# A hand-ordered attention and MLP kernel: GpSimd operations made to wait for VectorE's two-operand sums, one batch's q load issued by ScalarE, and a new written order

## The chip, the cores and the metric

The kernel runs on one core of a Trainium2 chip. The metric is the device time of one execution in microseconds (us), taken as the median of several runs. A core has five instruction queues that run side by side and meet at semaphores: TensorE (PE; its weight loads are listed as PEld), VectorE (DVE), ScalarE (ACT), GpSimd (POOL) and SyncE (SP). SP only issues transfers here; POOL and ACT can issue them too. Each queue works strictly in its own order.

## The reference, cut to what matters

```python
# q, k, v: (8 batches, 8 heads, 576 positions, 64)
kv  = einsum('bhsd,bhse->bhde', k, v)            # no softmax
o   = einsum('bhsd,bhde->bhse', q, kv)
x   = o / sqrt(mean(o*o, -1) + 1e-6) * g_norm    # then heads side by side: (8, 576, 512)

a1  = alpha1 * x + beta1
u   = x + lam * einsum('ts,bsd->btd', w_tok, a1) # mixes positions
a2  = alpha2 * u + beta2
out = u + lam * (maximum(a2 @ w_ch1, 0) @ w_ch2) # 512 -> 2048 -> 512
```

## The kernel before, in words

**Stages of one batch.** A batch b (0 to 7) is cut into four tiles of 128 positions, c = 0 to 3, and a tail of 64 positions; the tails of two batches share a tile, c = 4. The stages, by function:

- `load_kv` (L1393) and `load_q` (L1383): k and v by POOL's queue (L1395, L1399), q in four pieces by SP's queue (L1387) into the buffer `qs`, each after the landing that `landing` holds for the batch before.
- `kv` (L628): the k-v products on PE (L634, L640), gathered by ACT (L651) and DVE (L653).
- `qt_steady` (L1403): four pieces of q are transposed by DVE (L1405) and copied by ACT (L1408) to `qt`.
- `norm` (L717): PE multiplies `qt` by the k-v product (L725); ACT squares (L692), DVE sums (L695), ACT takes the root (L698), DVE inverts (L701), multiplies (L703) and writes x to `xm` (L710, or `xt` for a tail). POOL writes the bf16 tile `rm` (L713); for a tail DVE writes `rtl` (L708).
- `tok` (L805) and `tok_tail`: PE mixes positions (L808, L853) and needs all five tiles of `rm` and `rtl`; DVE adds the result to x (L818).
- `a2_dma` (L887): POOL rounds the tile to bf16 (`a2b`, L896; for batch 1 L905), and SP turns it by a transposing DMA (L909) into `a2m` (tail: `a2l`).
- `ch1` (L1018) and `ch1_tail`: the first product of the MLP on PE (L1020, L1034), with the rectifier on ACT (L913, L1042, L1051).
- The second product: `ch2` (L1075, PE L1081, DVE L1263 or L1257, POOL L1266) for batches 0 and 1; `strassen` (L1149) for the others. There DVE makes sums of two bf16 operands that both lie in SBUF (`sums`, `sums_late`, all through L1104), PE multiplies (L1142), ACT copies a partial result (`keep`, L1172), POOL adds it to x (L1175), DVE adds the last part (`last_add`, L1180), and the tile is stored (L1193, L1188). Batches 6 and 7 have such sums in their first product too (`pair`, L961, L983, L987).
- Once: `fold_w2` multiplies w_ch2 by lam (L1071), four slices by DVE and four by POOL; `fold_w1` (L1062) and `weight_sums` (L1104) follow on DVE.

**Order and waits.** Every operation gets a number as it is made. `ORDER` lists these numbers in the order in which they are put out, `a:3` naming the PSUM bank and `a+b` weaving two PE operations; so it sets the order of each of the five queues. `GATES` holds extra waits: `{774: 872}` makes operation 774 wait until 872 has ended. All other waits follow from what is read and written.

**Numbers that the text uses.** 237 to 240: the q load of batch 2. 390, 392, 394, 396 and 391, 393, 395, 397: its four transposes on DVE (L1405) and copies on ACT (L1408). 475, 479, 481, 483: rectifiers of batch 1 on ACT. 491: the first rectifier of batch 1 after the position mixing. 465, 467, 469: DVE's slices of `fold_w2`; 468: POOL's last; 379: POOL's last L1266. 1224: the first `keep` sum of batch 5 on POOL. 1227 to 1230: the four `sums_late` of batch 5 on DVE. 1285, 1301: `rm` tiles of batch 7 on POOL. 1231, 1242: `last_add` of batch 5. 1235, 1239: its other `keep` sums. 1309 and 1308: x and `rtl` of batch 7's tail. 1310: its first `tok`. 1085, 1087: the last two transposes of q of batch 6. 530 to 533: `fold_w1`. 563: the last L1257 of batch 1. 1577, 1590, 1594: the three `keep` sums of the tails, the last work of POOL; 1583: the last sum of L1104; 1567: the last `last_add` of batch 7 but the tails; 1597: the tails' L1180 that waits for 1594; 1575: a product of the tails.

Of the kernel before, what the change touches and what calls it, by code (L numbers as in the profile page):

```python
# [10 lines left out]
ACT = mybir.ActivationFunctionType  # L11
# [343 lines left out]
def bass_transnormer_attn__then__resmlp_affine_kernel(  # L355
# [15 lines left out]
    with ExitStack() as stack:  # L371
        P = Prog(nc, stack)
# [36 lines left out]
        a2b = sb("a2b", [128, 5, DM], BF16)  # L409
# [45 lines left out]
        def dcost(n, ns):  # L455
            return n * ns / 16000.0, float(ns)
# [13 lines left out]
             w=["idb"])  # L470
# [1080 lines left out]
```

## Time and profile before

| | before |
|---|---|
| median of 3 runs | 331.49 us (331.32 to 331.92) |
| the profiled execution | 332.1 us |
| its span, first to last instruction | 330.3 us |
| PE busy | 320.9 us (97%) |
| DVE busy | 252.1 us (76%) |
| ACT busy | 175.5 us (53%) |
| POOL busy | 146.4 us (44%) |
| granted TensorE clock | 1.0 throughout |

Durations in the text are of the profiled execution; what it says of runs is said of the median. Matmuls are pipelined, so the busy time of PE counts the drain of each; how far apart their starts lie is the better measure of whether it is held up. In a timeline the columns are start, time taken, queue, line, operation, tiles out<-in and shape, how many neighbours are merged in the row, and in brackets the idle time of the queue before it and what ended it. In the list of waits the three numbers are total us, times, and the longest.

### The profile page before, as it was taken

The numbers are of one execution on the slowest core, as the hardware profiler recorded it, in microseconds if no ns is written. First come the engines' busy times: TensorE is split into PE (matmuls) and PEld (weight loads), VectorE is DVE, ScalarE is ACT, GpSimd is POOL, SyncE is SP. The second block draws the span as 40 slices with busy tenths as digits, with TensorE's granted clock in tenths as the row PEclk, the third lists the DMA queues.
The fourth block names the chain that finished last, engine by engine and source line by source line (L and its number), as shares of the span: only waits on it lengthen the run. The fifth ranks groups of instructions, "written<-read, shape, count | busy, mean of one in ns | idle before, by whom it ended". The sixth has DMA issues, their size and how long they took to land.

```text
span 330.3 us, 6148 instructions
## 1 busy us (share of the span) xinstructions
PE 320.9 (97%) x2427; PEld 219.3 (66%) x2457; DVE 252.1 (76%) x443; ACT 175.5 (53%) x363; POOL 146.4 (44%) x147
## 2 busy tenths in 40 slices
PE   7999999998999999999999999999999899999996
PEld 7777664453766546786579874787658484557884
DVE  3596078775999998978985499789999677978534
ACT  5584672237734453619842585832784068873011
POOL 3599127899163473443258043564243600003232
PEclk9999999999999999999999999999999999999999
DMA  7999997999932896599059952596500250000314
GB/s 247 333 242 259 215 241 189 190 158 218 237 144 74 168 276 120 98 306 189 31 66 240 257 93 43 85 310 138 130 0 3 47 161 1 2 0 2 127 43 150
DMA packets 108532, 48.15 MB, mean 146 GB/s; under 512 B 82061, under 2 KB 101717, under 8 KB 108504
## 3 DMA queue, kind: packets, MB, share of 16 engines
q1 hardware_dynamic: 81520, 26.24, 33.8%
q0 software_dynamic: 26800, 21.38, 32.7%
q8 instruction: 19, 0.31, 0.4%
q10 hardware_dynamic: 184, 0.14, 0.2%
q14 instruction: 9, 0.07, 0.1%
HBM read 38.82 MB, written 9.44 MB: 146 GB/s over the span
## 4 chain that ended last, share of the span: by engine, by line
PE 71%; DVE 14%; ACT 5%; DMA 4%; issue 2%; SPq 2%; POOL 2%; DVEq 0%
PE ps L1142 21%; PE ps L1020 17%; PE ps L808 7%; PE ps L961 7%; PE ps L1081 6%; PE ps L1034 4%; PE ps L725 3%; DMA qs<-in_q_dram 2%; DVE ps L703 2%; POOL a2b L905 2%; DMA w<-in_k_dram 2%; PE ps L634 2%; ACT hh L913 1%; DVE small L695 1%; DVE qp L1405 1%
## 5 line engine op out<-in xcount | busy, mean ns | idle before, releaser
L1020 PE MATMUL ps<-a2m,w 128*128 128x512 bf16 x372 | 96.6, 385 | 0.6 <-DVE xm L1257 0.2
L713 POOL TENSOR_TENSOR rm<-xm,la_bc 128x512 bf16<-128x512 f32 x28 | 36.7, 1314 | 64.0 <-DVE xm L710 63.9
L1020 PEld LDWEIGHTS ps<-a2m,w 128*128 128x128 bf16 x384 | 35.9, 97 | 38.3 <-DVE xm L1257 0.6
L913 ACT ACTIVATE hh<-ps,b 128x512 bf16<-128x512 f32 x72 | 47.7, 685 | 13.1 <-PE ps L1020 9.4
L1175 POOL TENSOR_TENSOR xm<-xm,tmp 128x512 f32<-128x512 f32 x18 | 23.9, 1342 | 54.1 <-ACT tmp L1172 54.1
L725 PE MATMUL ps<-kvc,qt 128*128 128x128 f32 (+1 forms) x140 | 42.1, 404 | 1.4 <-ACT qt L1408 1.4
L1142 PE MATMUL ps<-w,hh 128*128 128x256 bf16 x344 | 40.2, 273 | 0.0
L1142 PEld LDWEIGHTS ps<-w,hh 128*128 128x128 bf16 x344 | 33.5, 98 | 5.4 <-issue 0.4
L1081 PE MATMUL ps<-w,hh 128*128 128x512 bf16 x138 | 36.5, 385 | 0.1
L634 PE MATMUL ps<-vr,kr 128*128 128x128 f32 x112 | 34.6, 410 | 0.0
L1172 ACT ACTIVATE tmp<-ps 128x512 f32<-128x512 f32 (+1 forms) x21 | 11.9, 566 | 38.4 <-PE ps L1142 38.4
L695 DVE TENSOR_REDUCE small<-sq 128x8 f32<-128x512 f32 (+1 forms) x35 | 23.5, 675 | 10.7 <-ACT sq L692 10.5
L808 PE MATMUL ps<-rm,wt 128*128 128x512 bf16 x106 | 29.1, 382 | 1.2 <-DVE rtl L708 1.1
L725 PEld LDWEIGHTS ps<-kvc,qt 128*128 128x128 f32 (+1 forms) x140 | 27.3, 196 | 4.1 <-ACT qt L1408 2.4
L896 POOL CAST a2b<-xm 128x512 bf16<-128x512 f32 x24 | 16.3, 678 | 30.8 <-DVE xm L818 30.8
L692 ACT ACTIVATE sq<-ps 128x512 f32<-128x512 f32 (+1 forms) x35 | 20.6, 596 | 16.1 <-PE ps L725 15.9
L1180 DVE TENSOR_TENSOR xm<-ps,xm 128x512 f32<-128x512 f32 x24 | 16.4, 686 | 15.7 <-PE ps L1142 8.2
L703 DVE TENSOR_TENSOR ps<-ps,small 128x512 f32<-128x512 f32 (+1 forms) x35 | 24.0, 692 | 0.5
L634 PEld LDWEIGHTS ps<-vr,kr 128*128 128x128 f32 x112 | 22.4, 200 | 1.5
L913 ACT ACTIVATE hh<-ps 128x512 bf16<-128x512 f32 x32 | 17.4, 601 | 10.6 <-PE ps L1020 10.4
L1408 ACT ACTIVATE qt<-qp 128x576 fp32r<-128x576 f32 x24 | 16.1, 683 | 13.0 <-DVE qp L1405 13.0
L1081 PEld LDWEIGHTS ps<-w,hh 128*128 128x128 bf16 x144 | 13.4, 97 | 13.8 <-issue 0.4
(199 smaller groups left out, 616.8 us busy)
## 6 DMA issues: line engine op xcount, KB each, us to landing
out_dram<-xm SPq DMA_DIRECT2D x32, 256.0 KB, 2.8
kr<-in_k_dram POOLq DMA_DIRECT2D x7, 1024.0 KB, 6.4
vr<-in_v_dram POOLq DMA_DIRECT2D x7, 1024.0 KB, 7.9
qs<-in_q_dram SPq DMA_DIRECT2D x24, 288.0 KB, 4.8
w<-in_moe_w_ch_dram POOLq DMA_DIRECT2D x8, 512.0 KB, 11.0
xm<-in_q_dram SPq DMA_DIRECT2D x8, 288.0 KB, 5.4
qs<-in_v_dram SPq DMA_DIRECT2D x4, 288.0 KB, 6.2
w<-in_k_dram SPq DMA_DIRECT2D x4, 288.0 KB, 6.2
```

The source lines that it names most:

```text
L634: P.mm("fill", 128, [lambda e, t=t, c=c, h=h, o=128 * (h % 4): e.matmul(t.ap()[:, o:o + 128], kr4[:, h, c:c + 2, :].rearrange("p c d -> p ...
L695: P.op("DVE", dve(n), lambda e: e.tensor_reduce(out=st, in_=sq[rs, s3, 0:nst, :], axis=AX.X, op=ALU.add), r=[("sq", s3)], w=[("sm", s4)])
L703: P.op("DVE", dve(n), lambda e: e.tensor_tensor(out=grp(ps()), in0=grp(ps()), in1=st[..., None].to_broadcast([rs.stop - rs.start, nst, DH] ...
L713: P.op("POOL", pool(n), lambda e: e.tensor_tensor(out=r, in0=x.rearrange("p h e -> p (h e)"), in1=la, op=ALU.mult), r=xks + ["la"], w=rks)
L725: P.mm("fill", 128, [lambda e, p=p: e.matmul(dst(p), qt[:, p, cs], kvc[:, i, p, :], start=(p == 0), stop=(p == 3)) for p in range(4)], r=[ ...
L808: P.mm("fill", 512, [lambda e, sc=sc: e.matmul(t.ap(), wt[:, sc if sc < 4 else tw(b), 128 * c:128 * c + 128], rsrc(b, sc, al), start=(sc = ...
L913: P.op("ACT", act(512, 0 if f is None else 1), lambda e: e.activation(dst, t.ap(), ACT.Relu, bias=0.0 if f is None else b1[:, f:f + 1]), r ...
L961: P.mm("main", 512, [lambda e, i=i: e.matmul(t.ap(), lhs[:, i, 128 * x + o:128 * x + o + 128], rhs[:, i, :], start=(first and i == 0), sto ...
L1020: P.mm("main", 512, [lambda e, dj=dj: e.matmul(t.ap(), w1[:, dj, 128 * fj:128 * fj + 128], a2m[:, b % 2, dj, :], start=(dj == 0), stop=(dj ...
L1081: P.mm("main", 512, [lambda e, fj=fj, t=t, c=c: e.matmul(t.ap(), (ht[:, fj, 128 * c:128 * c + 128] if c < 4 else hl[:, fj, :]), w2[:, fj, ...
L1142: P.mm("main", 256, [lambda e, c=c, fj=fj: e.matmul(t.ap()[:, 256 * c:256 * c + 256], at[:, fj, 128 * c:128 * c + 128], rhs(fj), start=(fi ...
L1175: P.op("POOL", pool(256 * n), lambda e, cs=cs, f=f: e.tensor_tensor(out=X[:, cs, f], in0=X[:, cs, f], in1=two(tmp[:, s]), op=ALU.add), r=x ...
```

## The change

Three things. `GATES` gets 40 entries: 39 operations of POOL (`keep` sums, `rm` tiles, `a2b` tiles, a slice of `fold_w2`, three L1266) each wait for the end of a DVE operation with two operands in SBUF that stands near them in the order (in one case an L987 with one operand), and the q load of batch 2 (237) waits for the landing of batch 1's third transposed tile (298). That q load is issued by ACT's queue instead of SP's. `landing` no longer keeps the landing of tile c = 3 or of a tail: later loads of k, v and q wait for tile c = 2. And `ORDER` is new from 238 on. POOL's DMA issues and DVE's other operations get no new wait.

```diff
@@ ORDER (from here to the end; only the first and a later stretch are shown)
-297 292 353:7 302 307 303 369 308 298 357 309 304 383:1+373 310 381:2+361 374 370 238 384+365 237
-239 382+490:3+496:0 366 240 462 464 491 470:4 367 385+486:5 463 476:7 388 399 378 471 389 488:3
...
+297 292 353:7 302 307 238 303 369 308 298 357 309 304 383:1+373 310 381:2+361 374 237 370 239
+384+365 240 382+490:3+496:0 366 462 464 491 470:4 367 385+486:5 463 476:7 388 399 378 471 389
...
@@ GATES
-    260, 399: 275, 586: 585, 587: 585, 588: 585, 589: 585, 747: 746, 748: 746, 749: 746, 750:
-    746, 940: 939, 941: 939, 942: 939, 943: 939, 1093: 1092, 1094: 1092, 1095: 1092, 1096:
-    1092}
+    260, 237: 298, 371: 465, 375: 465, 379: 467, 399: 275, 456: 654, 460: 654, 468: 467, 586:
+    585, 587: 585, 588: 585, 589: 585, 597: 656, 605: 651, 613: 651, 621: 656, 632: 657, 636:
+    652, 640: 652, 644: 652, 697: 703, 708: 703, 747: 746, 748: 746, 749: 746, 750: 746, 774:
+    872, 801: 873, 878: 884, 940: 939, 941: 939, 942: 939, 943: 939, 959: 911, 986: 1036, 990:
+    1037, 994: 1037, 1043: 1048, 1093: 1092, 1094: 1092, 1095: 1092, 1096: 1092, 1104: 1047,
+    1112: 1047, 1151: 1334, 1224: 1230, 1277: 1218, 1301: 1230, 1328: 1332, 1505: 1451, 1516:
+    1511, 1520: 1511, 1541: 1537, 1556: 1571, 1577: 1583, 1590: 1583, 1594: 1583}
@@ a2_dma
-            landing[b] = [P.dma(
+            o = P.dma(
                 "SP", "t%d" % c, 0.7, lambda e: e.dma_start_transpose(dst, a2b[:, c]),
-                r=[("a2b", c)], w=dk, issue=0.6)]
+                r=[("a2b", c)], w=dk, issue=0.6)
+            if c < 3:
+                landing[b] = [o]
@@ load_q
-                P.dma("SP", "q%d" % g, dcost(2304, 13.5), lambda e, hp=hp, j=j, g=g: e.dma_start(
+                P.dma("ACT" if b == 2 else "SP", "q%d" % g, dcost(2304, 13.5), lambda e, hp=hp, j=j, g=g: e.dma_start(
```

In the new order, on each queue: on ACT the four q issues stand behind the last L823 of batch 1 and ahead of 491, and rectifiers 481 and 483 go behind 395 and 397. On DVE 1308 goes ahead of 1309; the reciprocals L701 of batch 7's last two tiles stand just ahead of 1230, on which 1224 waits; 1242 goes ahead of batch 7's five L818; 1085 and 1087 go ahead of an L818 each; 530, 531, 533 and 563 go earlier among batch 3's `norm`; 1580 goes ahead of 1567. On SP three stores of batch 0 and 1 go in between and behind the q load of batch 3 instead of all behind it; some stores elsewhere change places with q loads. On POOL 1239 goes ahead of 1235, the keep of batch 4 ahead of batch 6's `rm`, one k load of batch 6 behind two `keep` sums, and loads change places among themselves. On PE some twenty products change places with a neighbour, the tails' 1575 going ahead of two products of batch 7.

123 rows, old and new, of the table ORDER are left out of this document.

## The prediction

> **What bounds the kernel now.** I read the page first (busy shares), then the list of waits for PE, then the timeline around each gap of PE, then what led to it in the chain of waits and the other queues' timelines.
>
> ```profile
> span 330.3 us, 6148 instructions
> PE 320.9 (97%) x2427; PEld 219.3 (66%) x2457; DVE 252.1 (76%) x443; ACT 175.5 (53%) x363; POOL 146.4 (44%) x147
> ```
>
> TensorE is the bound: 97% busy. The change takes no work from it. So only its gaps can be won, and the few per cent that are idle cap the gain. From the list of waits, those of PE that lie in the reordered part:
>
> ```profile
> PE ps L725 <- ACT qt L1408: 1.4, 2, 1.2
> PE ps L808 <- DVE rtl L708: 1.1, 1, 1.1
> PEld ps L1034 <- DMA a2l<-a2b: 0.3, 1, 0.3
> ```
>
> The timeline of PE at its four gaps, each with the row before it:
>
> ```profile
> 80.69 0.81 PE L1020 MATMUL ps<-a2m,w 128*128 128x512 bf16 x3
> 82.74 0.33 PE L725 MATMUL ps<-kvc,qt 128*128 128x128 f32 x1 [1.25 <-ACT qt L1408]
> ```
> ```profile
> 113.85 1.04 PE L1020 MATMUL ps<-a2m,w 128*128 128x512 bf16 x4
> 115.04 0.61 PE L1020 MATMUL ps<-a2m,w 128*128 128x512 bf16 x2 [0.15 <-DVE xm L1257]
> ```
> ```profile
> 205.17 1.03 PE L1020 MATMUL ps<-a2m,w 128*128 128x512 bf16 x4
> 206.37 0.33 PE L725 MATMUL ps<-kvc,qt 128*128 128x128 f32 x1 [0.17 <-ACT qt L1408]
> ```
> ```profile
> 255.10 1.04 PE L1142 MATMUL ps<-w,hh 128*128 128x256 bf16 x8
> 257.27 0.60 PE L808 MATMUL ps<-rm,wt 128*128 128x512 bf16 x2 [1.13 <-DVE rtl L708]
> ```
>
> The bracketed idle time is short of the loss, since each row ends with a drain. An L1020 starts every 0.216 us (three in 0.81 us, of which one lasts 0.38), an L1142 every 0.11 (eight in 1.04, one lasting 0.27). So PE could have gone on at 81.34, 114.72, 206.04 and 255.97. It went on at 82.74, 115.04, 206.37 and 257.27: **holes of 1.40, 0.32, 0.33 and 1.30 us**, 3.35 in all. That is the ceiling that I can name.
>
> **Part 1: GpSimd's 39 waits.** No engine gets more work. What they can win is DVE time: L1104 beside POOL's sums. First one group of L1104 (ns: shortest, median, longest), then PE's busy time in the stretch with its longest (span, sum of PE), then the timelines of DVE and POOL around the hole at 257.
>
> ```profile
> L1104 DVE TENSOR_TENSOR hh<-hh,hs x12: 412/683/4128, 138.7 to 323.5; 128x1024 bf16<-128x1024 bf16 x10, 128x512 bf16<-128x512 bf16 x2
> ```
> ```profile
> 118.00:150.00 32.00, 32.00 (x227) 21.84 (x226) 26.97 (x38) 15.47 (x27) 14.24 (x15) 1.00 0.91 193
> ```
> ```profile
> 249.67 0.69 DVE L1104 TENSOR_TENSOR hh<-hs,hh 128x1024 bf16<-128x1024 bf16 x1
> 250.28 2.36 DVE L1104 TENSOR_TENSOR hh<-hh,hs 128x1024 bf16<-128x1024 bf16 x2
> ```
> ```profile
> 250.00 1.49 POOL L1175 TENSOR_TENSOR xm<-xm,tmp 128x512 f32<-128x512 f32 x1 [2.22 <-ACT tmp L1172]
> 254.28 1.27 POOL L713 TENSOR_TENSOR rm<-xm,la_bc 128x512 bf16<-128x512 f32 x1 [2.79 <-DVE xm L710]
> ```
> ```profile
> 254.98 0.69 DVE L1180 TENSOR_TENSOR xm<-ps,xm 128x512 f32<-128x512 f32 x1
> 255.68 0.69 DVE L710 TENSOR_TENSOR xt<-ps,g_bc 64x512 f32<-64x512 f32 x1
> 256.30 0.69 DVE L708 TENSOR_TENSOR rtl<-ps,e_bc 64x512 bf16<-64x512 f32 x1
> ```
>
> A sum of 0.683 us (median) takes up to 4.128 beside POOL. But that one, at 139, lies in a stretch in which PE is busy for 32.00 of 32.00 us, and is worth nothing. Of the collisions only the one at 250 ends in a hole. Two sums starting 0.61 apart (249.67 to 250.28) would take 0.61 + 0.69 = 1.30; the row says 2.36: **1.06 us lost**, with POOL's 1224 running at 250.00 to 251.49. With the wait, 1224 starts behind 1230, which now ends at 252.64 - 1.06 + 0.20 (one reciprocal moved ahead of it) = 251.8. 1224 then ends at 251.8 + 1.27 = 253.1. What stands behind it on POOL is 1301, which was ready at 254.28, and is ready 1.06 earlier, 253.2: POOL is just free. It ends at 254.5. 1231 on DVE reads 1224's result at 254.98 - 1.06 = 253.9: no wait. The tail's `rtl` (1308), the last thing that PE waits for, ended at 256.99; less 1.06, less 0.62 for the place that it changes with 1309, that is 255.3. PE came 0.28 behind it (256.99 to 257.27), so it could go on at 255.6, and reaches the place at 255.97. The hole closes: **-1.30**; without the exchange of 1308 and 1309 it would be -1.06, and nothing if POOL's 1301 were late.
>
> The other waits have one answer each by group. The slice 468 of `fold_w2` waits for 467, and 379 stands behind it; both feed work that DVE reaches later. The `rm` and `a2b` waits before 250 end in tiles for which PE does not wait in the list above (its L808 waits only for DVE's `rtl`). Cost 0, bounded above by one POOL instruction, 1.27 us, where a tile were the last. At the end of the kernel there is no cover:
>
> ```profile
> 321.31 0.69 DVE L1180 TENSOR_TENSOR xm<-ps,xm 128x512 f32<-128x512 f32 x1 [1.06 <-PE ps L1142]
> ...
> 325.58 0.96 DVE L1180 TENSOR_TENSOR xt<-ps,xt 128x256 f32<-128x256 f32 x2 [1.36 <-POOL xt L1175]
> ```
> ```profile
> 323.95 1.59 POOL L1175 TENSOR_TENSOR xt<-xt,tmp 128x256 f32<-128x256 f32 x2 [1.02 <-ACT tmp L1172]
> ```
>
> 1567 (321.31) moves about 0.43 later, because product 1575 goes ahead of it on PE. Behind it are three half-size sums, 0.33 apart, so 1583 ends near 323.4. Now 1577, 1590 and 1594 follow back to back at 0.72 each: the last ends at 325.65 instead of 325.54. 1597 and PE's last product wait for that: **+0.10** (between 0 and 0.4).
>
> **Part 2: the q load of batch 2 by ACT's queue.**
>
> ```profile
> 60.38 5.24 SPq L909 DMA_TRANSPOSE a2m<-a2b  x4
> 65.66 1.27 SPq L909 DMA_TRANSPOSE a2l<-a2b  x1
> 66.97 5.31 SPq L1387 DMA_DIRECT2D qs<-in_q_dram  x4
> ```
> ```profile
> DMA to landing us min/median/max: 2.4/2.5/4.3
> ```
> ```profile
> 68.99 0.60 ACT L913 ACTIVATE hh<-ps 128x512 bf16<-128x512 f32 x1 [6.37 <-PE ps L1020]
> 71.81 0.38 ACT L651 ACTIVATE kvo<-ps 64x256 f32<-64x256 f32 x1 [2.21 <-PE ps L640]
> ```
> ```profile
> 70.65 6.86 DMA qs<-in_q_dram
> ...
> 80.09 1.46 ACT hh L913 x3
> 81.55 1.15 ACT qt L1408 x2
> ```
>
> The four issues stood on SP behind five transposing DMAs of L909 (the line below the SP rows is the issue-to-landing time of L909). The new wait is for the third: issued near 60.38 + 2 x 1.31 = 63.0, landed 2.5 later, 65.5. So they begin 1.45 us sooner than 66.97. The last piece took 6.86 us from 70.65 (chain of waits), as the next k and v loads came in on POOL; begun at 69.2 it lands at 76.1 with the same 6.86, and sooner if it is clear of them, instead of 77.5. On ACT rectifiers 481 and 483 leave the stretch that ends at 81.55 + 1.15 = 82.70 (three take 1.46, so 0.49 each): it ends at 81.7 even if the load lands no sooner, and at 80.3 or before with the earlier landing. PE comes there at 81.34. **-1.40**; -1.0 with the order alone.
>
> Price on ACT: it stands at the issues from 65.5 to 65.5 + 5.31 = 70.8 where it had 6.37 us idle before 68.99. Behind them are 491, ending at 71.4, and L651, not ready before 71.81. PE needs 491's bank again for its sixth `ch1` tile; the fourth ends with the L640 that released 71.81, the fifth takes 4 x 0.216, so near 72.5. Covered by 1.1 us. SP is free of the four; what is next there, q of batch 3, waits for the DVE transposes.
>
> **Part 3: loads wait for tile 2 instead of the last tile.** They begin one or two transposing DMAs (1.31 us each) sooner, and then share the engines with transposes that are still under way, whose landing goes from 2.5 to 4.3 us at worst. A PE wait for a transposed tile appears once in the list above, 0.3 us. Gain 0, cost between 0 and 1.8 us; I take 0, as that one wait is in batch 7, which no load follows.
>
> **Part 4: the order.** 1085 and 1087 each go ahead of an L818 on DVE, 0.6 us, more than the third hole: **-0.33**. 563 goes ahead of two steps of `norm`, 0.7 us, more than the hole at 114.72: **-0.30** (0 if DVE is later by as much for another reason).
>
> Such a reason would be `fold_w1`, just ahead of 563:
>
> ```profile
> 112.85 0.94 DVE L1062 TENSOR_SCALAR w<-w,ab 128x2048 bf16<-128x2048 bf16 x1
> ```
> ```profile
> 112.13 1.17 POOL L1395 DMA_DIRECT2D vr<-in_v_dram  x1
> ```
>
> The two ran side by side, and POOL's DMA issues get no wait. The Trainium skill ("SBUF — State Buffer", "Who interferes with whom") has a rule that speaks against the change here: a VectorE `tensor_scalar` can hold both ports that it shares with GpSimd, and then not only GpSimd's sums but also the descriptors of a DMA issued by GpSimd exclude it. By that rule this collision stays, and the term would be 0 instead of -0.30. The row neither bears it out nor excludes it, as no L1062 ran alone.
>
> The some twenty exchanges on PE have no row; bounds: 0 and another hole such as the largest, 1.4. I take **+0.3**, the size of the small holes, which are the usual ones here.
>
> **Sum:** -1.40 - 1.30 - 0.33 - 0.30 + 0.10 + 0.30 = -2.93 us, against the profiled execution's 332.1, which is 0.6 above the median. From 331.49: **328.6 us**.
>
> **Rivals.**
> - *The first hole stays.* The q pieces land no sooner and DVE or ACT work fills the stretch before `norm`. For it: DVE has `fold_w2` slices there. Against it: the order alone shortens ACT's stretch. 328.6 + 1.4 = 330.0 us.
> - *The waits only move the hole: no change.* POOL goes 1224, 1301, 1239 without a pause from 251.8, to 255.7 at best and 256.4 if 1224 and 1301 take 1.49 and 1.7; DVE's 1242 (there at about 256) now stands ahead of batch 7's five L818 and waits for 1239, and the a2l landing behind them is the one that PE waits for at 269 (0.3). If 1301 comes late on POOL, the hole at 257 opens again (1.30), and if 1239 is a POOL sum later than that allows (1.27), batch 7's L818 come later by it: 328.6 + 1.30 + 1.27 = 331.2 us.
> - *Slower: ACT is held by the issues.* Four q issues took far longer beside k and v loads:
>
> ```profile
> 115.39 9.29 SPq L1387 DMA_DIRECT2D qs<-in_q_dram  x4
> 213.97 11.01 SPq L1387 DMA_DIRECT2D qs<-in_q_dram  x4
> ```
>
>   On ACT every rectifier of batch 1 stands behind them. Up to 6.4 us PE feels nothing (71.9, then 491, against 72.5). Beyond that it loses one for one: at 9.29 us it is 2.9, which eats the whole gain, and that is the point from which it decides; at 11.01 it is 4.6, and 328.6 + 4.6 = 333.2 us. Against it: the next k and v loads stand on POOL behind batch 2's k-v products on PE, and the same four took 5.31 in this place.
>
> **How the numbers follow.** Forecast 0.62, first hole stays 0.12, no change 0.13, slower 0.13. A measurement of this kernel tells about 0.2%, 0.66 us. So faster 0.74, same 0.13, slower 0.13. The forecast's own range is 327.7 (the new order costs nothing and also closes gaps of 0.1 to 0.2 that I did not count) to 329.8 (+1.4 instead of +0.3). The range goes on to 331.3, with the first two rivals in it, and leaves out the third.
>
> **What would show it.** Right: no PE gap over 0.3 us at the first `norm` of batch 2 and at `tok` of batch 7; the two sums at 250 in 1.3 us; no L1104 over 1.1 us; ACT's four issues in 5 to 6 us. Wrong: a new PE wait on ACT's L913 near 72, on L1408 near 81, or on L808 for POOL's `rm`; a DVE wait for POOL's L1175 that feeds batch 7; transposes landing after 4 us with PE behind them.

## The result, and the profile after

The changed kernel takes 328.56 us (median; 328.33 to 329.46) where the kernel before takes 331.40 us (331.02 to 331.92): ratio 0.9919, 95% interval 0.9898 to 0.9941, so 2.8 us less. The head of the page of the changed kernel (span, then busy time by engine):

```profile
span 326.6 us, 6188 instructions
...
PE 321.1 (98%) x2457; PEld 219.4 (67%) x2457; DVE 242.8 (74%) x443; ACT 175.6 (54%) x363; POOL 141.5 (43%) x147
```

PE does the same work in a shorter span. VectorE is busy for 9.3 us less (252.1 before) and GpSimd for 4.9 less (146.4 before) with the same number of instructions each: the groups that shrink are the sums and roundings that no longer run into each other. VectorE's part alone is three times what the kernel gained. From the list of PE's waits:

```profile
PE ps L464 <- DVE fil L463: 1.1, 1, 1.1
PE ps L811 <- DVE rtl L711: 0.4, 1, 0.4
```

The first is the start of the kernel and was there before. The second is what is left of the hole at 257 us; the wait for `qt` is gone. PE's timeline at the four places where the prediction saw holes:

```profile
77.75 3.40 PE L1025 MATMUL ps<-a2m,w 128*128 128x512 bf16 x15
80.80 0.41 PE L728 MATMUL ps<-kvc,qt 128*128 128x128 f32 x1
...
111.64 4.58 PE L1025 MATMUL ps<-a2m,w 128*128 128x512 bf16 x20
...
201.86 1.89 PE L1025 MATMUL ps<-a2m,w 128*128 128x512 bf16 x8
203.52 0.33 PE L728 MATMUL ps<-kvc,qt 128*128 128x128 f32 x1
...
252.24 0.82 PE L1147 MATMUL ps<-w,hh 128*128 128x256 bf16 x6
253.41 1.04 PE L811 MATMUL ps<-rm,wt 128*128 128x512 bf16 x4 [0.36 <-DVE rtl L711]
```

The first three are closed: each row goes on where the one ahead of it ends, without a bracket. The fourth is half closed. Its cause stands in the timelines of DVE, then POOL, then ACT:

```profile
244.66 0.69 DVE L1109 TENSOR_TENSOR hh<-hh 128x1024 bf16<-128x1024 bf16 x1
246.18 0.69 DVE L1109 TENSOR_TENSOR hs<-hh 128x1024 bf16<-128x1024 bf16 x1 [0.83 <-ACT hh L918]
246.91 1.29 DVE L1109 TENSOR_TENSOR hh<-hs,hh 128x1024 bf16<-128x1024 bf16 x2
248.12 0.68 DVE L1109 TENSOR_TENSOR hh<-hh,hs 128x1024 bf16<-128x1024 bf16 x1
...
252.66 0.69 DVE L711 TENSOR_TENSOR rtl<-ps,e_bc 64x512 bf16<-64x512 f32 x1
```
```profile
249.93 1.27 POOL L1180 TENSOR_TENSOR xm<-xm,tmp 128x512 f32<-128x512 f32 x1 [5.24 <-DVE hh L1109]
251.26 1.27 POOL L716 TENSOR_TENSOR rm<-xm,la_bc 128x512 bf16<-128x512 f32 x1
```
```profile
245.46 0.69 ACT L918 ACTIVATE hh<-ps,b 128x512 bf16<-128x512 f32 x1
```

The collision is gone: no sum takes more than 0.69 us, POOL's 1224 (249.93) comes behind 1230 and 1301 right behind 1224. But the new order puts 1220 (246.18) ahead of 1227, and 1220 waits 0.83 us for ACT's rectifier 1184. With `rtl` PE gets its last operand at 253.35.

**How the runs are compared.** The executions differ by up to 2.3 us in the first 20 us, where PE waits for the first loads. All kernels here are the same up to PE's product 369 (a `ch2` product of batch 0; it starts at 62.35 us in the profile of before, at 61.99 in that of the changed kernel, and between 61.58 and 63.86 in the experiments), and behind it two kernels agree within about 0.01 us up to the first place that their edit touches. So each trace is measured from the start of 369 to the end of the span: 330.27 - 62.35 = 267.92 us before, 326.62 - 61.99 = 264.63 after, **-3.29**. The medians say -2.84. By medians every kernel here stands worse against before than by its trace, by 0.4 to 1.8 us, and before has one profiled execution, 0.6 above its median. The zero of this measure is therefore uncertain by a microsecond or so. The single executions of e4 and e5, which keep the old order, do follow that of before within 0.1 us outside the places that the text names for them, so these steps are no drift; but each kernel has one trace, and the reading by tenths is that of one execution each.

| kernel | order | GpSimd's waits | q of batch 2 | from 369 to the end, us | against before | ratio of whole times, 95% |
|---|---|---|---|---|---|---|
| before | old | none | SP | 267.92 | | |
| changed | new | 39 | ACT | 264.63 | -3.29 | 0.9898 to 0.9941 |
| e1 | new | none | ACT | 267.36 | -0.56 | 0.9989 to 1.0024 |
| e2 | new | 39 | SP | 265.12 | -2.80 | 0.9908 to 0.9952 |
| e13 | new | none | SP | 267.66 | -0.26 | 1.0003 to 1.0033 |
| e4 | old | 37 | SP | 266.59 | -1.33 | 0.9934 to 0.9981 |
| e5 | old | none | ACT | 266.94 | -0.98 | 0.9965 to 1.0016 |
| e11 | old | 37 | ACT | 264.97 | -2.95 | 0.9938 to 0.9979 |
| e6 | new | 9 | ACT | 264.85 | -3.07 | 0.9890 to 0.9947 |
| e3 | new, 1227 first | 39 | ACT | 264.07 | -3.85 | 0.9893 to 0.9939 |
| e10 | new, 1227 first | 10 | ACT | 264.25 | -3.67 | 0.9904 to 0.9955 |
| e9 | new, landing as before | 39 | ACT | 264.85 | -3.07 | 0.9915 to 0.9962 |
| e12 | new | 39 | ACT, 238 later | 264.77 | -3.15 | 0.9927 to 0.9971 |
| e8 | new | 39 | ACT, all later | 273.37 | +5.45 | 1.0136 to 1.0219 |

### The profile page after: what moved, and what is told of

Same layout as the page of the kernel before. It is cut to its first block, busy times and chain, and to the rows that moved or that the text cites. A ratio compares the mean times of both kernels' runs of the same rounds, so it can differ in the third digit from the quotient of the medians.

```text
span 326.6 us, 6188 instructions
## 1 busy us (share of the span) xinstructions
PE 321.1 (98%) x2457; PEld 219.4 (67%) x2457; DVE 242.8 (74%) x443; ACT 175.6 (54%) x363; POOL 141.5 (43%) x147
## 4 chain that ended last, share of the span: by engine, by line
PE 87%; DVE 6%; ACT 2%; DMA 2%; SPq 1%; issue 0%; POOL 0%; POOLq 0%
PE ps L1025 26%; PE ps L1147 20%; PE ps L1086 10%; PE ps L811 10%; PE ps L966 7%; PE ps L1039 4%; PE ps L728 3%; PE ps L637 2%; DMA qs<-in_v_dram 2%; PE ps L856 1%; DVE hh L1109 1%; DVE small L779 1%; PE ps L593 1%; SPq L480 1%; PE ps L876 1%; ACT hh L918 1%
## 5 line engine op out<-in xcount | busy, mean ns | idle before, releaser
L1025 PE MATMUL ps<-a2m,w 128*128 128x512 bf16 x384 | 98.5, 384 | 0.0
L716 POOL TENSOR_TENSOR rm<-xm,la_bc 128x512 bf16<-128x512 f32 x28 | 35.5, 1274 | 59.4 <-DVE xm L713 52.5
L1180 POOL TENSOR_TENSOR xm<-xm,tmp 128x512 f32<-128x512 f32 x18 | 23.1, 1293 | 62.2 <-DVE xm L992 33.3
L1147 PE MATMUL ps<-w,hh 128*128 128x256 bf16 x344 | 41.0, 273 | 0.0
L1086 PE MATMUL ps<-w,hh 128*128 128x512 bf16 x144 | 37.7, 385 | 0.0
L811 PE MATMUL ps<-rm,wt 128*128 128x512 bf16 x112 | 30.2, 382 | 0.4 <-DVE rtl L711 0.4
L899 POOL CAST a2b<-xm 128x512 bf16<-128x512 f32 x24 | 14.7, 612 | 33.7 <-DVE xm L821 28.5
L918 ACT ACTIVATE hh<-ps 128x512 bf16<-128x512 f32 x32 | 17.4, 597 | 11.4 <-PE ps L1025 11.3
```

The costliest lines, as they stand in the source:

```text
L716: P.op("POOL", pool(n), lambda e: e.tensor_tensor(out=r, in0=x.rearrange("p h e -> p (h e)"), in1=la, op=ALU.mult), r=xks + ["la"], w=rks)
L811: P.mm("fill", 512, [lambda e, sc=sc: e.matmul(t.ap(), wt[:, sc if sc < 4 else tw(b), 128 * c:128 * c + 128], rsrc(b, sc, al), start=(sc = ...
L918: P.op("ACT", act(512, 0 if f is None else 1), lambda e: e.activation(dst, t.ap(), ACT.Relu, bias=0.0 if f is None else b1[:, f:f + 1]), r ...
L1025: P.mm("main", 512, [lambda e, dj=dj: e.matmul(t.ap(), w1[:, dj, 128 * fj:128 * fj + 128], a2m[:, b % 2, dj, :], start=(dj == 0), stop=(dj ...
L1086: P.mm("main", 512, [lambda e, fj=fj, t=t, c=c: e.matmul(t.ap(), (ht[:, fj, 128 * c:128 * c + 128] if c < 4 else hl[:, fj, :]), w2[:, fj, ...
L1147: P.mm("main", 256, [lambda e, c=c, fj=fj: e.matmul(t.ap()[:, 256 * c:256 * c + 256], at[:, fj, 128 * c:128 * c + 128], rhs(fj), start=(fi ...
```

## The experiments

**e1: the changed kernel without the waits.**

```
 GATES = {..., 235: 260, 237: 298, 399: 275, ...}   # the 39 others out
```

> The changed kernel without the 39 waits of GpSimd; the new order, the q load by ACT's queue and its wait stay. Theory A (each part wins its own hole of PE): the waits are worth the collision at 250 us alone. Without them 1224 starts near 248.6 again, beside the last of the four VectorE sums, 1308 ends about 1.1 us later, and the hole of PE there grows from 0.5 to about 1.6 us: 329.6 us (+1.0 to the changed kernel's 328.56); the 10 us of longer VectorE sums that come back elsewhere cost nothing. Rival B (the order alone did it): 328.6, no hole larger than with the waits. Rival C (VectorE's total is what counts): 330.5 or more, with holes in several stages.

Measured: -0.56 instead of -3.29; the waits are worth 2.73 us in the new order. C is nearest in size, but the loss lies in a few places, as A has it, only in more of them than A named. First PE's timeline, then DVE's, then POOL's:

```profile
86.45 0.39 PE L1086 MATMUL ps<-w,hh 128*128 128x512 bf16 x1 [0.24 <-DVE w L1076]
...
216.46 2.21 PE L1147 MATMUL ps<-ab_bc,hh 128*128 128x256 bf16 x16
...
256.01 0.81 PE L811 MATMUL ps<-rm,wt 128*128 128x512 bf16 x3 [1.70 <-DVE rtl L711]
```
```profile
81.79 2.29 DVE L1076 TENSOR_TENSOR w<-w,lam_bc 128x1024 bf16<-128x1024 bf16 x1
...
85.19 1.21 DVE L1076 TENSOR_TENSOR w<-w,lam_bc 128x1024 bf16<-128x1024 bf16 x1
...
212.45 1.76 DVE L1109 TENSOR_TENSOR hh<-hs,hh 128x1024 bf16<-128x1024 bf16 x1
214.13 1.75 DVE L1109 TENSOR_TENSOR hh<-hh,hs 128x1024 bf16<-128x1024 bf16 x1
215.81 1.75 DVE L1109 TENSOR_TENSOR hh<-hs,hh 128x1024 bf16<-128x1024 bf16 x1
...
248.16 2.40 DVE L1109 TENSOR_TENSOR hh<-hs,hh 128x1024 bf16<-128x1024 bf16 x2
```
```profile
213.62 3.39 POOL L716 TENSOR_TENSOR rm<-xm,la_bc 128x512 bf16<-128x512 f32 x2
```

At 81.79 fold_w2's 467 takes 2.29 instead of 1.21 us, 469 behind it ends at 86.40, and PE waits for it: 0.62 us lost. At 212 to 219 four sums run beside POOL's; PE falls back by 0.8 us up to 226 (the sixteen products at 216.46 take 2.21 us, where the changed kernel takes 1.91), and the 0.22 that the changed kernel gains up to 245 us stays away too. At 248 the pair takes 2.40 instead of 1.29 us: 1.1 us. Together 2.7.

**e13: the new order alone.**

```
 GATES = {..., 237: 298, ...}                            # the 39 out, as in e1
-  P.dma("ACT" if b == 2 else "SP", "q%d" % g, ...
+  P.dma("SP", "q%d" % g, ...
```

> The changed kernel without the 39 waits and with batch 2's q load on SP's queue: the new order alone (with the loads' earlier landing). From product 369 to the end, 267.9 before. Theory A (additive: without waits the new order ends at 267.4; SP's issue among the transposes costs the 0.49 us that it cost with the waits): 267.8 to 267.9, no gain at all. Rival (the delay of PE at 68 us only fills the wait of 0.6 us at 86 us that is there without the waits): 267.3 to 267.4. Rival (the later q load opens the first hole as well): 268.5 or more.

Measured: 267.66, between the two; PE loses 0.34 at 68 us and nothing of it is given back at 86, so the additive reading holds, with a smaller term. The new order without the rest is worth next to nothing (-0.26, and by whole times 0.2% slower): it closes the holes at 82, 115 and 206, widens the one at 257 (the pair at 248 and the pause ahead of 1220 add up), and opens others at 88 and at 219 to 228.

**e4: the waits alone, in the old order.**

```
-GATES = {..., 399: 275, 586: 585, ...}
+GATES = {..., 371: 465, 375: 465, 379: 467, ..., 1224: 1230, ..., 1594: 1583}   # without 801, 1112, 237
```

> The kernel before with 37 of the 39 new waits of GpSimd and nothing else (two of them would stand the other way round in its order and are left out; the order on each engine is that of before). Theory A: the pair of VectorE sums at 250 us takes 1.3 us instead of 2.36, so rtl comes 1.06 us sooner and PE's hole at 257 us falls from 1.30 to 0.2 to 0.3 us: 330.4 us (331.4 less 1.0); VectorE's busy time falls by 8 to 10 us of which all but 1 us is worth nothing. Rival B (order alone): 331.4, as 1301 and 1239 come late on POOL. Rival C (the total counts): 329.5 or less.

Measured: -1.33. DVE's pair at 250:

```profile
249.45 1.34 DVE L1104 TENSOR_TENSOR hh<-hh,hs 128x1024 bf16<-128x1024 bf16 x2
```

1.34 instead of 2.36 us, and 1.02 of the 1.33 lie at `tok` of batch 7, as A says; 0.19 at 113 and 0.23 at 236 to 245 us come from other collisions, 0.2 is given back at 270. The first hole stays at 1.3.

**e5: the q load by ACT's queue alone, in the old order.**

```
-  P.dma("SP", "q%d" % g, ...
+  P.dma("ACT" if b == 2 else "SP", "q%d" % g, ...      # and 237 waits for 298
```

> The kernel before with batch 2's four q issues on ACT's queue, the first to be asked for behind transpose 298, and nothing else. Measured from PE's product 369 (before part 2) to the end of the span, as the starts of single executions differ: before 267.9 us, changed kernel 264.6. Theory A (landing and order each close a part of the first hole): q lands near 72 instead of 77.5 us, ACT no longer stands from 76.26 to 78.35 for it, but the rectifiers 481 and 483 still stand ahead of the third qt copy and are paced by PE; the last qt copy ends near 81.9, the hole falls from 1.4 to about 0.6: 267.1 us. Rival (only the order counts): 267.9. Rival (the landing alone is enough): 266.5.

Measured: -0.98, but not as A says. PE's timeline, then DVE's:

```profile
79.27 1.89 PE L1020 MATMUL ps<-a2m,w 128*128 128x512 bf16 x8
80.81 0.41 PE L725 MATMUL ps<-kvc,qt 128*128 128x128 f32 x1
...
86.86 0.39 PE L1081 MATMUL ps<-w,hh 128*128 128x512 bf16 x1 [0.24 <-DVE w L1071]
```
```profile
82.20 2.29 DVE L1071 TENSOR_TENSOR w<-w,lam_bc 128x1024 bf16<-128x1024 bf16 x1
```

The first hole closes whole, in the old order, so the landing alone is enough for it. PE then comes to fold_w2's slices 1.5 us sooner; 467 (82.20), slowed by POOL, delays 469, and PE loses 0.55 us there.

**e11: waits and q load together, in the old order.**

```
 GATES as in e4, and 237: 298
+  P.dma("ACT" if b == 2 else "SP", "q%d" % g, ...
```

> The kernel before, in its own order on every engine, with 37 of the 39 waits and batch 2's q issues by ACT's queue behind transpose 298. From product 369 to the end, 267.9 before. Theory A (the waits and the q load do nearly all, the new order hardly anything): the first hole closes (-1.5), the wait at 86 us that the q load alone left behind (+0.55) goes with the waits, and the hole at 257 falls to 0.3: 267.9 - 1.33 - 0.98 - 0.55 = 265.1 us, 0.5 above the changed kernel; the holes of 0.32 at 115 and 0.33 at 206 stay. Rival (the gains need the new order): 265.6 (the plain sum of the two alone) or more.

Measured: -2.95 where the two alone give -2.31: theory A, within 0.1. The wait at 86 us that the load uncovers is one that the waits remove. This is read from one trace each: by whole times (the ratios in the table) e11 is no better than e4, and each of the two is known to 0.2% (0.7 us) only. The new order adds 0.34 to this, but not by the two holes at 115 and 206 us alone. It wins 0.39 at 99 to 115 and 0.41 at 206, and it loses 0.47 at `tok` of batch 7: the old order has 1227 ahead of 1220, so that e11's VectorE has no pause for ACT there. The new order exchanges many more neighbours on ACT and VectorE than the description of the change names; the two traces differ for good only at these places.

**e2: the q load by SP's queue, in the new order.**

```
-  P.dma("ACT" if b == 2 else "SP", "q%d" % g, ...
+  P.dma("SP", "q%d" % g, ...
```

> The changed kernel with batch 2's q load on SP's queue again, at its new place in the order. Theory A1 (ACT's new order closes most of the first hole, the earlier landing the rest): q lands near 77 us, the two qt copies end near 81.7, PE comes near 81.3: hole of about 0.4 us, 329.0 us. Rival A2 (the earlier landing closes all of it): the hole of 1.4 us is back, 330.0 us. Rival A3 (the issues on ACT cost something): 328.3 us or less.

Measured: +0.49 against the changed kernel, but neither A1 nor A2: the first hole is closed with SP too, and that the median (329.02 us) is A1's number is luck. What is lost is lost at 68 us. SP's timeline, then PE's:

```profile
63.34 0.58 SPq L1392 DMA_DIRECT2D qs<-in_q_dram  x1
63.98 3.36 SPq L912 DMA_TRANSPOSE a2m<-a2b  x2
```
```profile
68.61 0.60 PE L1025 MATMUL ps<-a2m,w 128*128 128x512 bf16 x2 [0.31 <-DMA a2m<-a2b]
```

The new order has 238 between two transposes; on SP it holds up the ones behind it (one of them takes 2.05 us there instead of 1.28), and PE waits for a transposed tile. ACT's queue is what keeps the early issue out of their way. The load itself is early here, too, as only three of its issues stand behind the transposes; DVE's transposes of q wait for its last landing, in e2, then in before:

```profile
76.52 2.31 DVE L1410 STREAM_TRANSPOSE qp<-qs 128x576 f32<-128x576 f32 x3 [1.41 <-DMA qs<-in_q_dram]
```
```profile
77.53 2.31 DVE L1405 STREAM_TRANSPOSE qp<-qs 128x576 f32<-128x576 f32 x3 [2.97 <-DMA qs<-in_q_dram]
```

That is 13.9 us behind product 369 instead of 15.2. So the new order with the load on SP suffices for the hole, but by two things at once: the landing is 1.3 us earlier, and rectifiers leave the stretch of qt copies. What the rectifiers alone would do was not tried.

**e6 and e10: which waits.** e6 keeps nine of the 39, e10 keeps these and 1277 behind 1218, and has the exchange of e3.

```
+ e6:  371: 465, 375: 465, 379: 467, 468: 467, 1043: 1048, 1104: 1047, 1112: 1047, 1224: 1230, 1301: 1230
+ e10: these, 1277: 1218, and 1227 ahead of 1220
```

> The changed kernel with nine of the 39 waits of GpSimd: 371, 375 behind 465; 379, 468 behind 467; 1043 behind 1048; 1104, 1112 behind 1047; 1224, 1301 behind 1230. The other 30 are left out. From product 369 to the end: without any wait 267.4, with all 264.6. Theory A (the 2.7 us lie in three places, at 82 to 86, 212 to 219 and 248 to 253 us, where a VectorE sum beside GpSimd is the last thing that PE waits for): 264.6 to 264.9 us. Rival (the waits work by VectorE's total, of which these nine bring back only some 6 of 10 us): 265.5 or more.

> The changed kernel with ten of the 39 waits (the nine of the run before and 1277 behind 1218) and with VectorE's sum 1227 ahead of 1220. Theory A: the ten are all that pay, 1277 behind 1218 is the 0.22 us at 236 to 245 us that the nine left out, and the exchange closes the last hole: as the kernel with all 39 waits and the exchange, 264.1 us from PE's product 369 to the end (268 before, 264.6 changed), 0.9905 to 0.9915 of before. Rival (the 0.22 us have another cause): 264.3 to 264.4. Rival (the exchange leans on one of the 29 other waits): 264.6 or more.

Nine waits bring 2.51 of the 2.73 us: theory A in e6. The tenth was chosen wrong in e10: the same 0.22 us are missing again. DVE's timeline of e10, then of e3, which has all the waits, then POOL's of e10:

```profile
231.91 1.69 DVE L1109 TENSOR_TENSOR qs<-w 128x1024 bf16<-128x1024 bf16 x2
```
```profile
231.21 1.27 DVE L1109 TENSOR_TENSOR qs<-w 128x1024 bf16<-128x1024 bf16 x2
```
```profile
232.05 1.01 POOL L899 CAST a2b<-xm 128x512 bf16<-128x512 f32 x1 [1.30 <-DVE xm L821]
```

POOL's 1151 runs beside 1334 here; the wait of 1151 for 1334, among those left out, keeps them apart in e3 and in the changed kernel. That it is worth the 0.22 was not tried by itself.

**e3: 1227 ahead of 1220.**

```
-  ... 1184 1225:4 1297 1220 1223 1226 1229 1227 1232 ...
+  ... 1184 1225:4 1297 1227 1220 1223 1226 1229 1232 ...
```

> The changed kernel with VectorE's sum 1227 ahead of 1220 instead of two places behind it, and nothing else. Theory A (the 0.52 us hole that is left before tok of batch 7 comes from VectorE standing 0.8 us for ACT's rectifier 1184 ahead of 1220): 1227 fills that pause, the sums and 1308 end 0.7 us sooner, the hole closes: 328.0 to 328.1 us. Rival: POOL's 1224 (behind 1230) and 1301, or 1231 that reads 1224's result on VectorE ahead of 1308, set the end: 1308 moves less than the sums, and the time stays at 328.4 to 328.6 us.

Measured: 264.07, 0.56 less than the changed kernel: theory A. DVE's pause for ACT is filled:

```profile
244.85 0.69 DVE L1109 TENSOR_TENSOR hh<-hs,hh 128x1024 bf16<-128x1024 bf16 x1
245.77 0.69 DVE L1109 TENSOR_TENSOR hs<-hh 128x1024 bf16<-128x1024 bf16 x1 [0.23 <-ACT hh L918]
```

This is the best version by the trace. By medians (328.41 us; 0.9916 of before) it can't be told from the changed kernel.

**e8 and e12: the price of holding ACT.** In e8 all four issues stand behind fold_w2's 463 (it ends at 70.16), in e12 the first, too, stands behind transpose 298.

```
 e8:  ... 366 462 463 238 237 239 240 ... 491     GATES 238: 463
 e12: ... 298 238 357 ... 237 370 239 ...          GATES 238: 298
```

> The changed kernel with the four q issues on ACT held back further: they stand behind VectorE's fold_w2 slice 463, which ends near 70.2 us, instead of behind transpose 298 (66 us); 491 stands behind them on ACT as before. Theory A (the prediction's price: PE feels nothing as long as 491 ends by about 72.5 us, and loses one for one beyond that): issues from 70.2 to 73.5 to 75.0, 491 ends at 74.1 to 75.6, PE loses 1.6 to 3.1 us near 72: 266.2 to 267.7 us from product 369 to the end, against 264.6. Rival (ACT's rectifiers have more slack than that, or PE has other banks): 264.6 to 265.0.

> The changed kernel with the first of the four q issues (238) behind transpose 298 as well; in the changed kernel it waits for nothing and goes out at 61.7 us. Theory A (that early load only slows the transposes beside it, with none of them awaited by PE, and the last piece lands near 73 us, far ahead of its use): transposes land in 2.5 us again instead of up to 4.1, issues on ACT from 66 to 70, 491 ends near 70.8, 264.6 us from product 369 to the end, no hole at 72 or 82. Rival (ACT is held past 72.5 us, as where the four begin at 70.2): 265 to 268.

ACT's queue in e12, then in e8, with PE's timeline of e8:

```profile
67.05 5.37 ACTq L1392 DMA_DIRECT2D qs<-in_q_dram  x4
72.47 0.60 ACT L918 ACTIVATE hh<-ps 128x512 bf16<-128x512 f32 x1 [8.34 <-issue]
```
```profile
70.19 8.53 ACTq L1392 DMA_DIRECT2D qs<-in_q_dram  x4
78.76 0.60 ACT L918 ACTIVATE hh<-ps 128x512 bf16<-128x512 f32 x1 [16.54 <-issue]
```
```profile
79.41 2.31 PE L1025 MATMUL ps<-a2m,w 128*128 128x512 bf16 x5 [6.95 <-ACT hh L918]
```

The last issue of e8 in its chain of waits (start, us):

```profile
73.50 5.22 ACTq L1392
```

e12 loses nothing at 72 (0.14 us, near 267): held to 72.47, so that 491 ends 9.2 us behind its product 369, ACT is still early enough. In e8 the issues took 8.53 us, not the 3.3 to 4.8 that I expected; the k and v loads, which POOL issues from 71.67 to 73.98, were now under way. 491 ended 17.4 us behind 369, and PE, which stood 7.1 us, went on 0.05 later. So PE feels nothing up to 17.4 - 7.1 = 10.3 us behind 369. Beyond that it pays more than one for one here, as a second cost of 1.6 us follows, and it is PE's own clock. Two stretches behind the stand, with the busy time of PE, PEld, DVE, ACT and POOL, then the granted clock, DMA's share and GB/s:

```profile
79.40:82.70 3.30, 3.06 (x7) 1.16 (x9) 2.07 (x3) 3.24 (x7) 1.14 (x1) 0.51 0.90 135
82.70:90.00 7.30, 7.30 (x37) 3.45 (x36) 4.70 (x6) 6.72 (x14) 5.61 (x5) 1.00 0.37 73
```

After standing for 7 us PE works for 3.3 us at a granted clock of 0.51, and its products start 0.43 us apart instead of 0.216; then it has 1.00 again. The last q piece lands at 83.31, but PE does not wait for it. The Trainium skill ("DMA: Bandwidth & Descriptors", "Issuing engines are not separate DMA queues") says that the time to initiate a DMA is usually small beside the DMA. Here the last of the four held ACT's queue for 5.2 us and landed 9.8 us after it began: not small.

**e9: the loads wait for the last tile, as before.**

```
-            if c < 3:
-                landing[b] = [o]
+            landing[b] = [o]
```

> The changed kernel with the later loads waiting for the transposed last tile again, as before, instead of tile 2; nothing else. Theory A (part 3 is worth nothing, since every load lands before it is read): 264.6 us from product 369 to the end, within 0.15. Rival B (the loads of a later batch are late without it, by one or two transposing DMAs): 265.2 to 267.2, with PE waiting for qt, k or v at a norm or kv product. Rival C (the early loads slow the transposes): 264.0 to 264.4.

Measured: +0.22, a little outside A and far from B: 0.12 of it comes at 143 us, the rest near 265, and no wait for `qt`, k or v appears. The same place moves by 0.14 in e12, whose edit lies 200 us ahead of it, so that only the 0.12 can be put down to part 3.

## Why the prediction was right, point by point

The time was right (328.6 forecast, 328.56 measured), and so were three of the four holes. That the two numbers meet so closely is in part luck: 0.75 us too much was forecast at 257, and 0.7 of gain that was not foreseen and 0.4 of allowances that were not needed more than made up for it, to -3.29 by the trace; the medians say -2.84. The sum, term by term, with PE's lead over before in the trace:

| term | forecast, us | measured, us |
|---|---|---|
| first hole (82.7) | -1.40 | -1.51 |
| hole at 115, with its neighbours at 99 and 113 | -0.30 | -0.59 |
| 236 to 245 us | not foreseen | -0.23 |
| hole at 206 | -0.33 | -0.40 |
| hole at 257 | -1.30 | -0.55 |
| tail | +0.10 | 0.0 |
| the new order's own waits | +0.30 | 0.0 (but see 257) |
| sum | -2.93 | -3.29 |

**The hole at 257 was mis-sized twice.** It was never 1.30 us. Before's first product of `tok` has lost its record; its PE timeline shows three products ahead of the first `rtl`, where the changed kernel's row above has four:

```profile
257.27 0.81 PE L808 MATMUL ps<-rm,wt 128*128 128x512 bf16 x3 [1.13 <-DVE rtl L708]
257.91 0.38 PE L808 MATMUL ps<-rtl,wt 128*128 128x512 bf16 x1
```

PE's first weight load there, whose records are complete, starts at 257.04. With 0.216 for the missing one the hole was 1.08, and e10, which closes it, gains just that there. And of these only 0.55 came, since I followed the collision through POOL and the tail, but not what the new order puts ahead of 1227: 1220, whose wait for ACT (0.83 us) takes the place of the collision. e3 shows it: with 1227 first, the other 0.53 come. The price of the collision itself, -1.06, was right in the old order (e4: -1.02).

**That the other waits cost 0 and gain nothing is the step that failed.** I priced each wait by the holes of the trace before, where only the collision at 250 ends in one. In the old order that is nearly true (e4: 1.02 of 1.33 us). In the new order the waits are worth 2.73 us (e1). At 86 us the reason is shown: 467 beside POOL costs nothing as long as the first hole stands 4 us ahead of it, and 0.55 to 0.62 us once it is closed (e5, e1), as PE then comes sooner. The 0.8 us at 212 to 226 are likely of the same kind, but not shown to be: e5, where PE is 1 us ahead of before, loses nothing there, and the new order also has more collisions (four long sums in e1, two in e5). The allowance of +0.30 for waits of the new order came out at 0 only because the 39 waits are in it, and because its one wait that is left, the 0.47 us of 1220, is counted at 257.

**The first hole: the size was right, the division is open.** I had the order alone at -1.0 and the landing as the rest. e5 shows that the landing alone closes it whole. e2 closes it with the load on SP, but there the landing is 1.3 us earlier as well, so that -1.0 for the order alone is neither borne out nor refuted. The load's queue is worth 0.49 us in the new order for another reason, the transposes behind it on SP.

**The issues on ACT.** I had all four behind 298, from 65.5 to 70.8. In the changed kernel 238 stands ahead of 237 on ACT and waits for nothing; the last three take 3.3 us:

```profile
61.68 7.74 ACTq L1392 DMA_DIRECT2D qs<-in_q_dram  x4
69.47 0.60 ACT L918 ACTIVATE hh<-ps 128x512 bf16<-128x512 f32 x1 [7.20 <-PE ps L1025]
```

e12 is the kernel that I priced: 5.37 us of issues, and no harm. The slower rival's mechanism is real (e8), and its point of decision was right: 10.3 us behind product 369 against 72.5 - 62.35 = 10.15 forecast. Its price was not: PE lost 8.7 us for 7.1 us of standing, as the clock fell. As far as e12 and e8 show, what kept it away is that the issues begin ahead of the k and v loads.

**The hole at 115.** The prediction held open that this term is 0, because `fold_w1` runs beside POOL's load issues, and it said that no L1062 ran alone. One did: before's first (108.78) has no work of POOL beside it and takes 0.74 us; the four take 0.74, 0.93, 0.74 and 0.94. The collision is still there in the changed kernel (0.74 alone at 105.85, 1.07 at 107.25 beside the issues), and yet the hole is closed. In e9 all four take 0.74 or 0.75, and PE comes there no sooner. So this collision costs nothing; of the 0.59 in the table, 0.19 come by the waits alone (e4).

**"no L1104 over 1.1 us" was wrong.** One is left; DVE, then POOL:

```profile
214.95 1.77 DVE L1109 TENSOR_TENSOR hh<-hh,hs 128x1024 bf16<-128x1024 bf16 x1
```
```profile
214.53 1.65 POOL L1180 TENSOR_TENSOR xm<-xm,tmp 128x512 f32<-128x512 f32 x1 [5.52 <-DVE hh L1109]
```

1043 waits for 1048 but not for 1047 behind it. No wait of PE follows from this one in the list of its waits.

Still open: which part of the difference between -2.84 by medians and -3.29 by traces belongs to the start of the kernel and which to the one profiled execution of before.

## What to carry to other kernels

A hole list prices an edit only in the schedule that it was read from: when one edit brings the bottleneck engine forward, go to the next collision or late operand behind it and price that too, since an edit worth nothing today may be what keeps the other's gain (here, by the traces, -1.33 and -0.98 apart, -2.95 together, and an order worth -0.26 by itself). Compare traces from the last instruction that all variants share; then tenths of a microsecond can be placed where medians scatter by one. An issue on an engine that has work of its own costs its queue time, and that depends on which other loads are under way; if the bottleneck engine stands for long, its clock can fall, too (e8).

## What the hardware showed that I had not expected

- Beside POOL, VectorE's sum and POOL's both grow: in e1 DVE's sums, 0.68 us alone, start every 1.68 us at 212 to 217, and POOL's take 3.39 / 2 = 1.7 instead of 1.27. The Trainium skill ("SBUF — State Buffer", "Who interferes with whom") says that the ports which the two engines share are an exclusive lock, and that a VectorE instruction with two SBUF inputs contends with a GpSimd instruction that reads SBUF. If each held them for its whole instruction, a pair would take 0.68 + 1.27 = 1.95 us, an estimate from this case's durations. The rows agree that both are slowed, and show less than full turns.
- Four issues of the same q load took 5.37 us in e12 and 8.53 us 3 to 5 us later in e8.
- After PE had stood for 7 us in e8, its granted clock was 0.51 for 3.3 us.
- PE's records are not complete: 2427 of 2457 in before, and one was the first product behind a hole, which made that hole look 0.22 us longer. PEld had all 2457.
